# The remaining half of a nested product, with the low halves of probabilities kept in place

## Chip, cores and metric

One core of a Trainium2 chip. The metric is the device time of one execution in microseconds, the median of several runs. Five engines matter: TensorE (PE; its weight loads are listed as PEld), VectorE (DVE), ScalarE (ACT), GpSimd (POOL), and SyncE (SP), which issues all DMAs here.

## The reference

Two branches read the same `x` (2048 tokens, 576 features, float32) and are mixed by a gate per token:

```python
g = _sigmoid((x * gate_w).sum(-1, keepdims=True))
a = _A_ref(x, A_wq, A_wk, A_wv, A_wo, A_beta)   # 32 heads of 18, four segments of 512 tokens:
                                                # causal softmax inside a segment, plus a memory
                                                # read from the segments before it, then @ wo
b = _B_ref(x, B_w_gate, B_w_up, B_w_down)       # (gelu(x @ w_gate) * (x @ w_up)) @ w_down
return g * a + (1 - g) * b                      # w_gate, w_up: 576 x 4608; w_down: 4608 x 576
```

## The kernel before

**Numbers.** All large products run on TensorE in float16. Each operand is written as a high half and a low half (value minus high half); a product is three matmuls, high-high, high-low and low-high. ACT makes the high halves (an activation with `Copy`), and POOL or DVE makes the low halves by subtraction.

**Stages.** First come the projections to queries, keys and values and the memory of the segments (to about 208 us). Then the main loop, to about 1460 us: 72 calls of `step(v)`, in which the gated network and the attention run side by side. A tail applies `wo` and stores the result.

**The gated network.** The 4608 hidden columns form 36 blocks `f` of 128, and the tokens form four chunks of 512. `step(v)` treats block `f = v // 2` for the chunk pair `p = v % 2` (chunks 0 and 1, or 2 and 3). Inside a step the gate and up products for two chunks and two halves of the 576 features (256 features each, and a rest of 64) are done as a 2 x 2 block product in the Winograd form, with seven products instead of eight: `product(...)` with the weight parts A11, A12, A22, S1 to S4. They go to the PSUM banks V, X (bank "G") and Y (bank "U"). Two blocks form a pair `fb = v // 4`, and `i4 = v % 4` counts the steps of one turn: step 0 is the even block with chunks 0 and 1, step 1 the even block with chunks 2 and 3, steps 2 and 3 the odd block.

**The nested term.** One of the seven products, A12 times the second half of the features, is itself taken over two neighbouring blocks (even and odd `f`) and two halves of the chunk (256 tokens), again in seven products instead of eight: `nested(...)`, line 380, each three matmuls of 256 columns. Five of the seven run in the even block's step and two in the odd block's. In the kernel before this is done for the chunk pair 2 and 3 alone (`p == NP`, with `NP = 1`); the pair 0 and 1 does the whole `product(X, f, A12, x1, 2, 6)` in both steps. The sums of the nested form come back through a tile `nest_u[p]` on DVE: five operations of 256 columns in the even step (lines 1384 to 1388), two of 512 columns in the odd step (1397 and 1398), where the plain path has one copy of 512 columns (1402). The first block pair (`fb = 0`) does not nest.

**Weights of the next blocks**, prepared during the steps. POOL scales them (`scale_g`, `scale_up`, `scale_d`, lines 304, 310 and 425 by the profile), forms the Winograd sums (`sums_g`, lines 401 to 405), the nested sums (`nest_sums`, line 324, and a third one, line 421) and the low halves (`low_g`, line 417, `nest_low`, line 337, `low_d`, line 433); ACT makes the high halves. Lines of helpers are those of their last statement in the profile.

**Down products.** `chains` and `down` (line 1222) multiply the hidden values of the pair before by `w_down` (tile `paird`) in the gaps of a step, and DVE adds each into `acc` (line 1230).

**Attention.** Unit `a` is one head in one segment of 512 tokens; `step(v)` with `k = v - 4` starts the scores of units 2k and 2k + 1. `scores` gives four products (query blocks 3 to 0 of 128 rows, with up to 512 keys). DVE adds the mask, finds the maximum and writes the float32 row tile `pf` (line 1133, called `put` in the step, piece by piece: 1, 0, 3, 2). ACT takes the exponentials in place (`powers`, line 1146). `pair_rows` makes the halves: ACT the high half, POOL the low half (line 1157), both into a tile `ph` of two parts. `turn_rows` transposes both by DMA (line 1163), and `values` (line 1177) multiplies by the value rows. There are two `pf` and two `ph` buffers, so unit a + 2 uses those of unit a again.

**Order.** The order of instructions on PE, ACT, DVE and POOL is the order of the program text (`manual_schedule`). Each of these engines runs its list in that order and stops at an instruction whose inputs or target are not ready. The order of SP's DMAs is set by the framework.

Of the kernel before, what the change touches and what calls it, by code (L numbers as in the profile page):

```python
# [18 lines left out]
P = 128  # L19
# [4 lines left out]
L = 512  # L24
# [5 lines left out]
NP = 1  # L30
# [7 lines left out]
GB = 18  # L38
# [8 lines left out]
def kernel(ctx: ExitStack, tc: tile.TileContext, xs, wqk, wv, wo, wgu, wd, beta, out):  # L47
# [264 lines left out]
    A_11, A_12, A_22, N3, N1, N2, N4 = 2, 3, 3, 17, 17, 18, 19  # L312
# [94 lines left out]
    def high_g(f, b):  # L407
        if f < NF and not b:
            pair_g[f] = pair_tile(f)
        for p in parts_g(f, b):  # L410
            act.activation(spot(f, *p, 0), raw_g[f][:, p[0] : p[1]], AF.Copy)  # L411
            if b and f % 2 == 0 and f and p[0] == 0:
                nest_high(f)

    def low_g(f, b):
        for p in parts_g(f, b):
            pool.tensor_tensor(spot(f, *p, 1), raw_g[f][:, p[0] : p[1]], spot(f, *p, 0), OP.subtract)  # L417
            if b and f % 2 == 0 and f and p[0] == 0:
# [650 lines left out]
    with tc.tile_pool(name="keep", bufs=2, side="right", reuse_waits="tile") as kp, ExitStack() as tail:  # L1069
# [7 lines left out]
        home.update(a=ap_, n=stay.enter_context(tc.tile_pool(name="nest", bufs=1, reuse_waits="tile")))  # L1077
# [38 lines left out]
        COL = [0, P, 3 * P, 6 * P, 10 * P]  # L1116
# [3 lines left out]
        def scores(a):  # L1120
# [4 lines left out]
            prob[a] = ap_.tile([P, 10 * P], F32, name="pf", bufs=2)  # L1125
# [6 lines left out]
            def piece(qi):  # L1132
                dve.tensor_tensor_reduce(prob[a][:, COL[qi] : COL[qi + 1]], out[qi], mask[:, L - (qi + 1) * P :],  # L1133
# [4 lines left out]
        def powers(a):  # L1138
# [5 lines left out]
            for qi in (3, 0, 2, 1):  # L1144
                r = p[:, COL[qi] : COL[qi + 1]]
                act.activation(r, r, AF.Exp, bias=b[:, qi : qi + 1], scale=esc[:, 0, c : c + 1])  # L1146

        def pair_rows(a, i):

            p = prob[a]  # L1150
            if i == 0:
                pairs16[a] = ap_.tile([P, 2, 10 * P], F16, name="ph", bufs=2)
                turned_p[a] = ap_.tile([P, 20, P], F16, name="pt", bufs=2)
            h = pairs16[a]
            cols = (slice(6 * P, 10 * P), slice(0, 6 * P))[i]
            act.activation(h[:, 0, cols], p[:, cols], AF.Copy)  # L1156
            pool.tensor_tensor(h[:, 1, cols], p[:, cols], h[:, 0, cols], OP.subtract)  # L1157

        def turn_rows(a):
            prob.pop(a)  # L1160
            t, h = turned_p[a], pairs16.pop(a)
            for i in range(2):
                sp.dma_start(t[:, 10 * i : 10 * i + 10], h[:, i], transpose=True)
# [112 lines left out]
        def weights_first(fb, i4):  # L1276
# [3 lines left out]
            if i4 == 1 and fb:  # L1280
                sums_g(n0 + 1)
            if i4 == 2 and fb:
                scale_g(n0 + 2)
                scale_d(n0)
            if i4 == 3 and fb:
                sums_g(n0 + 2)
                scale_d(n0 + 1)

        def weights_high(fb, i4):
            n0 = 2 * fb  # L1290
            high_g(n0 + 1 + i4 // 2, i4 % 2)
            if i4 == 0:
                nest_high(n0 + 1)
            if i4 >= 2:
                high_d(n0 + i4 - 2)

        def weights_low(fb, i4):
            n0 = 2 * fb
            low_g(n0 + 1 + i4 // 2, i4 % 2)
            if i4 == 0:  # L1300
                nest_low(n0 + 1)
            if i4 >= 2:
                low_d(n0 + i4 - 2)
# [47 lines left out]
        def step(v):  # L1351
# [15 lines left out]
            if v == 3:  # L1367
                high_g(2, 1)
                low_g(2, 1)
            if v in (1, 3 + NP):  # L1370
                nest_high_x(NP, v > 1)
# [3 lines left out]
            if fb and p == NP and f % 2 == 0:  # L1375
# [3 lines left out]
                nested(X[:, n1], f, N1, p, "t1", True)  # L1379
                nested(X[:, n0], f, A_11, p, "b11")  # L1380
# [8 lines left out]
            elif fb and p == NP:  # L1389
# [9 lines left out]
            else:  # L1399
                product(X, f, A11, x1, 0, 4, True)  # L1400
                put(2 * k - 1, 3)
# [3 lines left out]
            if v != 4 and (p != NP or f % 2 == 0):  # L1405
# [20 lines left out]
            if v == 0:  # L1426
                nest_load(NP)
# [27 lines left out]
            if v in (1, 3 + NP):  # L1455
                nest_low_x(NP, v > 1)
# [4 lines left out]
            if v == 0 or fb > 1 and i4 == 1:  # L1461
# [9 lines left out]
            if not fb or p != NP:  # L1471
# [8 lines left out]
            if v == 5:  # L1480
                scales(2)
                scales_out(2)
                scale_up(5)
# [329 lines left out]
```

## Time and profile before

| | |
|---|---|
| median of 3 runs (lowest to highest) | 1566.31 us (1565.99 to 1567.05) |
| the profiled execution, its own time | 1566.07 us |
| span of its trace | 1564.3 us |
| granted TensorE clock | 1.00 |
| busy: DVE, ACT, POOL | 1198.3, 1184.2, 1292.5 us |
| mean traffic of the DMA queues | 134 GB/s, 472452 packets |

In the profile a timeline row reads: start, duration, engine, line, operation, target <- sources, shapes, count, and in brackets the idle time of the engine before it with what ended it. PE rows overlap, since a matmul's duration includes the way through the array; how fast PE goes is read from start to start. A wait row reads: engine, line <- what it waited for: us in total, times, longest. Shares of busy time are averages over stages with different limits. A main-loop turn of four steps takes about 73 us, and the loop is very regular, so one turn stands for seventeen.

### The profile page before, as it was taken

To read this page: it belongs to the slowest core of one execution; us is meant where nothing else is said; L and a number is where in the kernel's file an instruction comes from. 1 tells how busy PE (TensorE), PEld (TensorE's weight loads), DVE (VectorE), ACT (ScalarE), POOL (GpSimd) and SP (SyncE) were. 2 spreads that over 40 slices of the span, in tenths; PEclk is the share of its full clock that TensorE was granted. 3 is DMA by queue.
4 is the path that set the end of the run, shared out by engine and by line. 5 is a ranking of instruction groups with operands and counts; after the bars stand their busy time and mean duration, and the time that the engine had idled before them with its cause. 6 is when DMAs were issued, how large, how long until landed. Compare 5 with 4: busy or idle time off the path is not lost.

```text
span 1564.3 us, 33336 instructions
## 1 busy us (share of the span) xinstructions
PE 1555.5 (99%) x12042; PEld 939.8 (60%) x12043; DVE 1198.3 (77%) x3111; ACT 1184.2 (76%) x2035; POOL 1292.5 (83%) x1309
## 2 busy tenths in 40 slices
PE   9999999999999999999999999999999999999999
PEld 5665655555565555556555555656555556555577
DVE  6788975777878777778787787878787878787665
ACT  7567544888888888887888888888887888876421
POOL 3545776989898989898898989898989898898697
PEclk9999999999999999999999999999999999999999
DMA  7533341787878698978878998989797989884654
GB/s 240 208 131 122 126 136 38 123 135 125 136 128 154 117 144 123 148 122 134 134 132 128 135 139 134 146 122 158 123 139 127 153 118 145 128 136 90 132 111 137
DMA packets 472452, 209.55 MB, mean 134 GB/s; under 512 B 427616, under 2 KB 437344, under 8 KB 471776
## 3 DMA queue, kind: packets, MB, share of 16 engines
q1 hardware_dynamic: 472288, 207.44, 73.7%
q8 instruction: 94, 1.54, 0.4%
q14 instruction: 70, 0.57, 0.1%
HBM read 91.51 MB, written 27.26 MB: 76 GB/s over the span
## 4 chain that ended last, share of the span: by engine, by line
PE 54%; POOL 26%; ACT 12%; issue 6%; DVE 2%; DMA 1%; SPq 0%; POOLq 0%; DVEq 0%
PE dn L1222 13%; PE U L1262 11%; POOL ph L1157 5%; PE V L1262 5%; POOL hh L1249 5%; POOL raw L304 4%; POOL rawd L425 3%; ACT pf L1146 3%; POOL pairg L417 3%; ACT L1146 3%; PE st L440 3%; PE G L1262 2%; PE dn L447 2%; PE pv L1177 1%; ACT gl L1252 1%
## 5 line engine op out<-in xcount | busy, mean ns | idle before, releaser
L1222 PE MATMUL dn<-paird,hh 128*128 128x288 f16 x3396 | 478.8, 286 | 3.2 <-POOL paird L433 3.0
L1157 POOL TENSOR_TENSOR ph<-pf,ph 128x512 f16<-128x512 f32 (+1 forms) x256 | 353.9, 1404 | 114.8 <-ACT ph L1156 108.0
L1262 PEld LDWEIGHTS <-pairg 128*128 128x128 f16 x2820 | 264.0, 98 | 279.0 <-issue 18.0
L1222 PEld LDWEIGHTS <-hh 128*128 128x128 f16 x3456 | 332.1, 98 | 151.9 <-issue 24.5
L1230 DVE SCALAR_TENSOR_TENSOR acc<-dn,ev,acc 128x288 f32<-128x288 f32 x534 | 274.5, 515 | 57.9 <-PE dn L1222 48.0
L1146 ACT ACTIVATE pf<-pf,mb,esc 128x512 f32<-128x512 f32 (+3 forms) x512 | 293.0, 642 | 5.8
L1262 PE MATMUL U<-xt,pairg 128*128 128x512 f16 x864 | 209.9, 379 | 0.0
L417 POOL TENSOR_TENSOR pairg<-raw,pairg 128x640 f16<-128x640 f32 (+2 forms) x144 | 176.5, 1242 | 2.7 <-ACT pairg L411 2.5
L1249 POOL TENSOR_TENSOR hh<-gl,hh 128x512 f16<-128x512 f32 x144 | 164.5, 1163 | 11.5 <-ACT hh L1248 11.5
L1156 ACT ACTIVATE ph<-pf 128x512 f16<-128x512 f32 (+1 forms) x256 | 172.4, 720 | 0.0
L1133 DVE CUSTOM_DVE_ANT_0 pf<-st,mask 128x512 f32<-128x512 f32 (+1 forms) x256 | 157.2, 614 | 0.0
L1262 PE MATMUL U<-x,pairg 128*128 128x512 f16 x636 | 154.6, 379 | 0.1
L411 ACT ACTIVATE pairg<-raw 128x640 f16<-128x640 f32 (+2 forms) x144 | 89.4, 646 | 75.2 <-POOL raw L405 55.6
L1449 DVE COPY gl<-U 128x512 f32<-128x512 f32 x72 | 49.6, 689 | 115.8 <-POOL hh L1249 78.0
L1252 ACT ACTIVATE gl<-gl,sc 128x512 f32<-128x512 f32 x144 | 96.6, 715 | 34.8 <-DVE gl L1491 18.5
L1133 DVE CUSTOM_DVE_ANT_0 pf<-dn,mask 128x256 f32<-128x256 f32 (+1 forms) x192 | 67.2, 375 | 69.0 <-PE dn L1130 68.9
L304 POOL TENSOR_SCALAR raw<-raw,sc 128x640 f32<-128x640 f32 x72 | 118.7, 1661 | 0.0
L1262 PE MATMUL G<-x,pairg 128*128 128x512 f16 x456 | 110.8, 379 | 0.0
L1262 PE MATMUL V<-xt,pairg 128*128 128x512 f16 x432 | 105.7, 381 | 0.0
L1262 PE MATMUL V<-x,pairg 128*128 128x512 f16 x432 | 104.8, 378 | 0.0
L1143 ACT ACTIVATE mb<-mx,esc 128x4 f32<-128x4 f32 x128 | 37.3, 291 | 79.1 <-DVE mx L1133 79.1
L1248 ACT ACTIVATE hh<-gl 128x512 f16<-128x512 f32 x144 | 82.6, 615 | 16.1 <-DVE gl L1244 16.1
(354 smaller groups left out, 2913.8 us busy)
## 6 DMA issues: line engine op xcount, KB each, us to landing
raw<-in_wgu_dram SPq DMA_DIRECT2D x36, 640.0 KB
rawd<-in_wd_dram SPq DMA_DIRECT2D x36, 288.0 KB
qk<-stage SPq DMA_DIRECT2D x36, 256.0 KB
qt<-qk SPq DMA_DIRECT2D x128, 72.0 KB
kt<-qk SPq DMA_DIRECT2D x128, 72.0 KB
vp<-vstage SPq DMA_DIRECT2D x16, 296.0 KB
vt<-vp SPq DMA_DIRECT2D x16, 296.0 KB
qt<-qk SPq DMA_DIRECT2D x128, 36.0 KB
```

The source lines that it names most:

```text
L304: pool.tensor_scalar(r, r, scl[f // 2][0][:, 0:1], None, OP.mult)
L411: act.activation(spot(f, *p, 0), raw_g[f][:, p[0] : p[1]], AF.Copy)
L417: pool.tensor_tensor(spot(f, *p, 1), raw_g[f][:, p[0] : p[1]], spot(f, *p, 0), OP.subtract)
L1133: dve.tensor_tensor_reduce(prob[a][:, COL[qi] : COL[qi + 1]], out[qi], mask[:, L - (qi + 1) * P :], 1.0, -3e38, OP.add, OP.max, mx[a][:, q ...
L1146: act.activation(r, r, AF.Exp, bias=b[:, qi : qi + 1], scale=esc[:, 0, c : c + 1])
L1156: act.activation(h[:, 0, cols], p[:, cols], AF.Copy)
L1157: pool.tensor_tensor(h[:, 1, cols], p[:, cols], h[:, 0, cols], OP.subtract)
L1222: pe.matmul(o[:, :NH], hh[:, a, q * P : (q + 1) * P], w[:, b, n * NH : (n + 1) * NH], start=i == 0, stop=i == 5)
L1230: dve.scalar_tensor_tensor(av, o[:, :NH], ev, av, OP.mult, OP.add)
L1249: pool.tensor_tensor(hh[:, 1], t, hh[:, 0], OP.subtract)
L1252: act.activation(t, o, AF.Gelu_apprx_tanh, scale=scl[f // 2][0][:, 2 + c : 3 + c])
L1262: pe.matmul(o, w[:, i, (a + k) * P : (a + k + 1) * P], x[:, b + k], start=start and k == 0 and i == 0 and b == h, stop=k == 1 and i == 1, ...
```

## The change

1. The nested form is used for both chunk pairs. The constant `NP` goes, and with it the plain path in all block pairs but the first. Chunks 0 and 1 get their own words (`nest_load`, `nest_form`, `nest_high_x`, `nest_low_x` for p = 0 and 1) and their own tiles. In an odd block the nested weight sum N3 is written over the part of A12 that nothing reads any more (`N3 = 2`, `GB = 17`).
2. The low half of the probabilities is written into the first half of the bytes of `pf`, in place, so that `ph` has one part. The columns of `pf` are reversed: query block 3 lies first and block 0 last. The low half is transposed first, then the high half.
3. The order on POOL and ACT: `scale_d` for both blocks goes to the middle of step 1, behind `scales_out` and `scale_up`; the sums of the odd block go from step 1 to the end of step 0; in step 3 the second block's down weights and the nested halves are made between the two parts of `high_g` and `low_g`, and the third nested sum comes last.

```diff
-NP = 1
-GB = 18
+GB = 17
...
-    A_11, A_12, A_22, N3, N1, N2, N4 = 2, 3, 3, 17, 17, 18, 19
+    A_11, A_12, A_22, N3, N1, N2, N4 = 2, 3, 3, 2, 17, 18, 19
...
+    def nest_third(f):
+        if f < NF:
+            s3 = nest_w[f + 1] = nest_u[1][:, NL : NL + P]
+            pool.tensor_tensor(s3, raw_g[f + 1][:, KW + 3 * P : KW + 4 * P], nest_w[f][:, P : 2 * P], OP.subtract)
...
-        r = nest_x[p, "r"] = home["a"].tile([P, 10 * P], F32, name="pf", bufs=2)
+        r = nest_x[p, "r"] = home["p"][p]
...
-    def low_g(f, b):
+    def low_g(f, b, between=lambda: None):
+        if f >= NF:
+            between()
         for p in parts_g(f, b):
             pool.tensor_tensor(spot(f, *p, 1), raw_g[f][:, p[0] : p[1]], spot(f, *p, 0), OP.subtract)
-            if b and f % 2 == 0 and f and p[0] == 0:
-                nest_low(f)
-                s3 = nest_w[f + 1] = nest_u[NP][:, NL : NL + P]
-                pool.tensor_tensor(s3, raw_g[f + 1][:, KW + 3 * P : KW + 4 * P], nest_w[f][:, P : 2 * P], OP.subtract)
+            if p[0] == 0 and b:
+                between()
...
-        home.update(a=ap_, n=stay.enter_context(tc.tile_pool(name="nest", bufs=1, reuse_waits="tile")))
+        home.update(p=[ap_.tile([P, 10 * P], F32, name=f"pf{i}", bufs=1) for i in range(2)], n=stay.enter_context(tc.tile_pool(name="nest", bufs=1, reuse_waits="tile")))
...
-        COL = [0, P, 3 * P, 6 * P, 10 * P]
+        COL = [9 * P, 7 * P, 4 * P, 0]
...
-            prob[a] = ap_.tile([P, 10 * P], F32, name="pf", bufs=2)
+            prob[a] = home["p"][a % 2]
...
-            for qi in (3, 0, 2, 1):
+            for qi in (3, 2, 1, 0):
...
-                pairs16[a] = ap_.tile([P, 2, 10 * P], F16, name="ph", bufs=2)
+                pairs16[a] = ap_.tile([P, 10 * P], F16, name="ph", bufs=2)
...
-            cols = (slice(6 * P, 10 * P), slice(0, 6 * P))[i]
-            act.activation(h[:, 0, cols], p[:, cols], AF.Copy)
-            pool.tensor_tensor(h[:, 1, cols], p[:, cols], h[:, 0, cols], OP.subtract)
+            cols = (slice(0, 4 * P), slice(4 * P, 10 * P))[i]
+            act.activation(h[:, cols], p[:, cols], AF.Copy)
+            pool.tensor_tensor(p.bitcast(F16)[:, cols], p[:, cols], h[:, cols], OP.subtract)
...
-            prob.pop(a)
-            t, h = turned_p[a], pairs16.pop(a)
-            for i in range(2):
-                sp.dma_start(t[:, 10 * i : 10 * i + 10], h[:, i], transpose=True)
+            t = turned_p[a]
+            for i, h in ((1, prob.pop(a).bitcast(F16)[:, : 10 * P]), (0, pairs16.pop(a))):
+                sp.dma_start(t[:, 10 * i : 10 * i + 10], h, transpose=True)
...
-            if i4 == 1 and fb:
-                sums_g(n0 + 1)
             if i4 == 2 and fb:
                 scale_g(n0 + 2)
-                scale_d(n0)
             if i4 == 3 and fb:
                 sums_g(n0 + 2)
-                scale_d(n0 + 1)
...
-            low_g(n0 + 1 + i4 // 2, i4 % 2)
+            low_g(n0 + 1 + i4 // 2, i4 % 2, lambda: (low_d(n0 + 1), nest_low(n0 + 2)) if i4 == 3 else None)
             if i4 == 0:
                 nest_low(n0 + 1)
-            if i4 >= 2:
-                low_d(n0 + i4 - 2)
+                sums_g(n0 + 1)
+            if i4 == 2:
+                low_d(n0)
+            if i4 == 3:
+                nest_third(n0 + 2)
...
-            if v in (1, 3 + NP):
-                nest_high_x(NP, v > 1)
+            if 1 <= v < 5:
+                nest_high_x((v - 1) % 2, v > 2)
...
-            if fb and p == NP and f % 2 == 0:
+            if fb and f % 2 == 0:
...
-                nested(X[:, n1], f, N1, p, "t1", True)
-                nested(X[:, n0], f, A_11, p, "b11")
+                nested(X[:, n0], f, A_11, p, "b11", True)
+                nested(X[:, n1], f, N1, p, "t1")
...
-            elif fb and p == NP:
+            elif fb:
...
-                nest_load(NP)
+                for n in range(2):
+                    nest_load(n)
...
                     scale_up(2 * fb + 3)
+                    scale_d(2 * fb)
+                    scale_d(2 * fb + 1)
                 else:
-                    nest_form(NP)
+                    nest_form(0)
...
                 hidden_pair(f, c, g0)
+                if v == 1:
+                    nest_form(1)
                 ahead[v + 1] = first_product(v + 1)
```

`high_g` and `weights_high` change as `low_g` and `weights_low` do, for ACT.

More of the change, by code (lines that the diff above doesn't have):

```diff
@@ L1132, in piece @@
             def piece(qi):
-                dve.tensor_tensor_reduce(prob[a][:, COL[qi] : COL[qi + 1]], out[qi], mask[:, L - (qi + 1) * P :],
+                dve.tensor_tensor_reduce(prob[a][:, COL[qi] : COL[qi] + (qi + 1) * P], out[qi], mask[:, L - (qi + 1) * P :],
                                          1.0, -3e38, OP.add, OP.max, mx[a][:, qi : qi + 1])
@@ L1404, in step @@
                 scale_result()
-            if v != 4 and (p != NP or f % 2 == 0):
+            if v != 4 and i4 < 2:
                 some(fb - 1, early[:1])
@@ L1483, in step @@
                 scale_up(5)
+                scale_d(2)
+                scale_d(3)
             product(Y, f, S1, t, 0, 2)
```

26 lines of the change are left out of this document (15 added, 11 removed).

## Prediction

> **What bounds the kernel now.** I read the page first (busy shares), then a table of windows cut at the steps of the main loop, then PE's list of waits, then the timelines of PE, POOL, DVE and SP over the same four steps.
>
> ```profile
> span 1564.3 us, 33336 instructions
> PE 1555.5 (99%) x12042; PEld 939.8 (60%) x12043; DVE 1198.3 (77%) x3111; ACT 1184.2 (76%) x2035; POOL 1292.5 (83%) x1309
> ```
>
> TensorE is busy all the time, so a microsecond is won only where PE has fewer columns to push, or where it stands still inside that 99%. The windows are cut where each step's first product (into V) starts. In order they are step 3 of one turn of the loop (odd block, chunks 2 and 3), then steps 0 (even block, chunks 0 and 1), 1 (even, 2 and 3) and 2 (odd, 0 and 1) of the next.
>
> ```profile
> 597.56:615.16 17.60, 17.60 (x150) 10.60 (x147) 13.89 (x38) 14.49 (x25) 17.07 (x19) 1.00 0.82 116
> 615.16:633.76 18.60, 18.41 (x149) 10.59 (x146) 13.52 (x37) 17.11 (x32) 16.55 (x15) 1.00 0.86 132
> 633.76:652.39 18.63, 18.63 (x159) 11.51 (x157) 16.94 (x48) 14.54 (x24) 14.97 (x20) 1.00 1.14 157
> 652.39:670.63 18.24, 18.24 (x149) 10.60 (x146) 13.07 (x37) 15.85 (x28) 16.62 (x13) 1.00 0.75 130
> ```
>
> Columns: length, then busy us of PE, PEld, DVE, ACT, POOL, then clock and DMA. A turn is 73.07 us at full clock (1.00). Steps 0 and 2 run the same products now (149 matmuls each), yet step 0 is 0.36 us longer. Steps 1 and 3 already have the nested term that the change brings to steps 0 and 2, so they show what steps 0 and 2 should become. POOL is 17.07 us busy out of 17.60 in step 3: it, not DVE or ACT, is the engine next to PE.
>
> ```profile
> PE dn L1222 <- POOL paird L433: 3.0, 16, 0.2
> ```
>
> PE's only repeated wait, once per turn from the second turn on: the down chain needs the low half of a block's down weights.
>
> **The change, part by part.**
>
> *The term in seven products, chunks 0 and 1.*
>
> ```profile
> 618.61 0.41 PE L1222 MATMUL dn<-paird,hh 128*128 128x288 f16 x2 [0.19 <-POOL paird L433]
> ...
> 635.07 0.82 PE L380 MATMUL G<-x,pairg 128*128 128x256 f16 x6
> ...
> 636.05 1.46 PE L1262 MATMUL U<-x,pairg 128*128 128x512 f16 x6
> ...
> 653.70 1.46 PE L1262 MATMUL G<-x,pairg 128*128 128x512 f16 x6
> 654.99 0.90 PE L1222 MATMUL dn<-paird,hh 128*128 128x288 f16 x6
> ```
>
> Six matmuls of 512 columns take 654.99 - 653.70 = 1.29 us, 0.215 each. From 635.07 to 636.05 PE runs nine nested matmuls of 256 columns (six into G, three into dn): 0.98 us, 0.109 each, so half the columns cost half the time. Step 0 loses one product (1.29) and gets five nested ones, 15 matmuls (1.64): +0.34. Step 2 loses 1.29 and gets two, six matmuls (0.65): -0.64. The windows agree: step 3 (nested) is 17.60 against 18.24 for step 2 (not), and step 1 against step 2 is +0.39, a little of it the scale sum that only step 1 has. Net -0.30 us a turn; the nested path runs for 17 of the 18 block pairs (not the first): **-5.1 us**. Nine weight loads more per turn lie beside matmuls (PEld 11.51 us of 18.63 in step 1).
>
> DVE pays:
>
> ```profile
> 618.14 0.69 DVE L1402 COPY U<-G 128x512 f32<-128x512 f32 x1
> ...
> 622.48 0.69 DVE L1449 COPY gl<-U 128x512 f32<-128x512 f32 x1 [2.44 <-POOL hh L1249]
> ...
> 637.01 0.42 DVE L1384 COPY nu<-G 128x256 f32<-128x256 f32 x1
> ...
> 639.00 0.43 DVE L1388 TENSOR_TENSOR G<-U,nu 128x256 f32<-128x256 f32 x1
> ```
>
> In step 0 one copy of 0.69 becomes five operations from 637.01 to 639.43, 2.4 us: +1.7. In step 2 it becomes two additions of 512 columns, +0.7. In front of L1449 DVE idles 2.44 us in step 0, and the added work falls just there, ahead of the same copy; DVE then holds 15.2 of 18.6 us, less than step 1's 16.94, where PE waits for nothing. Priced at nothing; without that cover it would be up to 1.7 us a turn, 29 in all. ACT's exponentials of the odd unit start up to 1.6 us later in step 0, as they do in step 1.
>
> *POOL's order.* Weight products of POOL around step 3, and its two gaps:
>
> ```profile
> 605.54 0.73 POOL L401 TENSOR_TENSOR raw<-raw 128x256 f32<-128x256 f32 x1
> ...
> 608.65 0.46 POOL L405 TENSOR_TENSOR raw<-raw 128x128 f32<-128x128 f32 x1
> 609.08 1.73 POOL L425 TENSOR_SCALAR rawd<-rawd,sc 128x576 f32<-128x576 f32 x1
> 610.78 2.77 POOL L1157 TENSOR_TENSOR ph<-pf,ph 128x512 f16<-128x512 f32 x2
> 613.49 1.42 POOL L417 TENSOR_TENSOR pairg<-raw,pairg 128x640 f16<-128x640 f32 x1
> 614.86 0.93 POOL L337 TENSOR_TENSOR pairg<-junk,pairg 128x384 f16<-128x384 f32 x1
> ...
> 617.27 1.29 POOL L433 TENSOR_TENSOR paird<-rawd,paird 128x576 f16<-128x576 f32 x1
> 618.56 2.77 POOL L1157 TENSOR_TENSOR ph<-pf,ph 128x512 f16<-128x512 f32 x2
> ...
> 636.78 2.77 POOL L1157 TENSOR_TENSOR ph<-pf,ph 128x512 f16<-128x512 f32 x2 [4.92 <-ACT ph L1156]
> ...
> 655.42 2.76 POOL L1157 TENSOR_TENSOR ph<-pf,ph 128x512 f16<-128x512 f32 x2 [1.62 <-ACT ph L1156]
> ```
>
> POOL's work does not grow. The down weights' scaling (L425, 1.73 us) leaves steps 2 and 3 and goes, both together (3.5 us), to the end of step 1. The five weight sums (L401 to L405, 605.54 to 609.11, 3.6 us) go from the head of step 1 to the end of step 0, into the gap of 4.92 us, which still holds them if the odd unit comes 0.9 us later. The head of step 1 is free 3.6 us earlier, so the 3.5 us behind it plus the gap of 1.62 fit ahead of 655.42. In step 3 everything behind L425 comes 1.73 earlier, and L433 moves ahead of the nested and second weight parts. Its end goes from 618.56 to 613.49 + 1.42 - 1.73 + 1.29 = 614.5, three microseconds before the down chain asks. The wait goes: 0.36 us (step 0 against step 2), 16 times: **-5.8 us**.
>
> What is late next: the nested low halves of an even block (L337), which PE needed in step 1 until now and needs in step 0 then, about 616.8 (615.16 + 1.3 for the first product + three nested matmuls). They end at 614.5 + 0.93 = 615.4; slack 1.4 us. Should the 1.73 not come through, 617.1, a wait of 0.3.
>
> *Low halves over the probabilities.* No engine gains or loses an instruction; POOL's subtraction keeps its shape. What changes is the wait: DVE writes the next unit's scores into that buffer, and for the first pieces of the row (query blocks 3 and 2) it must now wait for the transpose of the low half to land, where it waited for POOL. Pieces 1 and 0 lie behind the low halves' bytes. Behind the waiting DVE instruction stand the down chains' sums and the hidden products, so PE soon pays. SP now issues the low half first; with that the high half, ready earlier, also waits for POOL.
>
> ```profile
> 627.45 0.42 DVE L1133 CUSTOM_DVE_ANT_0 pf<-dn,mask 128x256 f32<-128x256 f32 x1 [1.59 <-PE dn L1130]
> ...
> 629.64 0.68 DVE L1133 CUSTOM_DVE_ANT_0 pf<-st,mask 128x512 f32<-128x512 f32 x1
> ```
>
> ```profile
> 622.05 5.51 SPq L1163 DMA_TRANSPOSE pt<-ph  x2
> ```
>
> ```profile
> DMA  6111189991111111111169999900002999131159
> ```
>
> POOL is done with a unit at 618.56 + 2.77 = 621.33, SP issues its two transposes from 622.05, and DVE writes piece 3 two units on at 629.64. The digits are DMA's busy tenths from 622 to 632 us, 0.25 each: the first transpose works around 623.5 to 624.25 and 626.75 to 628.25, the second to 630.5. So the transpose that is issued first has moved its bytes by 628.25, 1.4 us before DVE needs the buffer. How long from the last byte to the waiting engine?
>
> ```profile
> 1467.70 2.27 POOL L1628 TENSOR_TENSOR pairg<-ot 128x512 f32<-128x512 f16 x2 [4.22 <-DMA ot<-orow]
> ```
>
> ```profile
> DMA  6946999985100000499999999998179861669862
> ```
>
> Here POOL does wait for a transpose. The digits run from 1460 us; the activity of its two transposes ends at about 1467.0, and POOL starts 0.7 us later. So 628.25 + 0.7 = 628.95 against 629.64: nothing, with 0.7 us to spare. The Trainium skill (page "DMA: Bandwidth & Descriptors", section "Anatomy of one DMA") says otherwise: about 2 us of fixed cost, most of it behind the last byte until the write is confirmed. By that the buffer would be free at 630.25, 0.6 us late; the trace has 0.7 us where the page has up to 2, on a transpose too, so I go by the trace.
>
> In the odd units of step 3 POOL ends 1.73 earlier, which pays for the low half's way.
>
> *The first block pair.* Chunks 0 and 1 need their own words: one more load of 512 KB (behind the first, needed 15 us later) and four more subtractions on POOL in step 1 of the first pair, put ahead of that step's last low half.
>
> ```profile
> 218.33 1.69 POOL L349 TENSOR_TENSOR nu<-pf 128x256 f32<-128x256 f32 x1 [0.31 <-DMA pf<-in_xs_dram]
> ...
> 221.71 0.72 POOL L349 TENSOR_TENSOR pf<-pf 128x256 f32<-128x256 f32 x1
> ...
> 232.99 2.27 POOL L1249 TENSOR_TENSOR hh<-gl,hh 128x512 f16<-128x512 f32 x2
> ```
>
> ```profile
> 235.74 0.69 DVE L1449 COPY gl<-U 128x512 f32<-128x512 f32 x1 [2.39 <-POOL junk L324]
> ```
>
> ```profile
> 237.20 1.46 PE L1262 MATMUL U<-xt,pairg 128*128 128x512 f16 x6
> ```
>
> The same four took 218.33 to 222.43, 4.1 us; at 0.73 each with small gaps 3.1. They go between the two low halves at 232.99, whose second ends then at 238.4 to 239.4 instead of 235.26. It frees the buffer that DVE's copy at 235.74 writes, and PE's product at 237.20 needs that copy done: 239.1 to 240.1, a stall of 1.9 to 2.9, once. I take **+2.4 us**, since the one slow row of the four may come again. The few ACT and DVE operations on those words fall into idle time there.
>
> **Sum.** -5.1 - 5.8 + 2.4 = -8.5. The profiled execution took 1566.07 us (span 1564.3 and 1.8 around it), 0.24 under the median: 1557.6 in its terms, **1557.8 us** as a median.
>
> **Rivals.**
>
> *Late low half (slower).* One mechanism: piece 3 waits on DVE for the transpose. It decides at 0.7 us more than I reckon from issue to landing. Against it: the rows above, and loads in the queue were already in them. For it: SP's order is not written out by the kernel, so loads may stand ahead of the transposes, and single issues take 3 us where two together took 5.51. If 1 us is added in one unit of each step, DVE is 0.3 late; 64 steps with attention make 19 us: 1577. At 0.14 us a step (8.5 / 64) the gain is gone. Were the wait set for the whole buffer and not for its overlapping bytes, piece 1 at 627.45 would wait for 628.95, 1.5 us, over 90 us in all. Against that:
>
> ```profile
> 660.40 3.74 POOL L304 TENSOR_SCALAR raw<-raw,sc 128x640 f32<-128x640 f32 x2
> ```
>
> ```profile
> 662.42 0.72 ACT L411 ACTIVATE pairg<-raw 128x640 f16<-128x640 f32 x1
> ```
>
> ACT reads the first part of a tile at 662.42 while POOL writes its second until 664.14: waits go by parts.
>
> *The wait moves (no change).* POOL does not run ahead, and the nested low halves are late in step 0 instead of the down weights. Against: in step 3 its work falls from 17.07 to 15.3 us of 17.6. If the wait stays as it is, 5.8 come back: 1563.6; with 0.3 more for the nested ones, 17 times, 1568. I say 1563 to 1568.
>
> *No start cost (faster).* If the stall in the first pair is covered: 1555.4.
>
> **How the numbers follow.** About 0.2%, 3.1 us, is what a measurement of this kernel can tell from no change. Forecast with its bounds (1553.5 to 1563): 0.72, the start cost of nothing to 2.9 and half the wait in it. Wait moves: 0.12, nearly all within 0.2%. Late low half: 0.13 slower; a few more for the moved wait at its worst. So faster 0.73, same 0.12, slower 0.15. The range runs from 1553.5 to 1571, through the moved wait and the mild end of the late half.
>
> **What would show it.** Right: steps 0 to 3 of 18.6, 18.6, 17.6 and 17.6 us; no wait of PE for L433; the gap of 4.92 on POOL filled with the sums; one PE stall of about 2 us near 237. Wrong: DVE's score pieces (L1133) waiting for DMA, with every step longer by the same amount; PE waiting for L337; or steps 0 and 2 not differing as steps 1 and 3 do.

## The result, and the profile after

The changed kernel takes 1556.84 us (median of 6 runs, 1556.42 to 1557.48); the kernel before took 1565.99 beside it (6 runs). The ratio is 0.9941, with a 95% interval of 0.9930 to 0.9953: faster by 9.15 us, where 8.5 were forecast. In every later set of runs the median of the kernel before was 1565.68 to 1566.03, so times of different sets can be compared to a few tenths of a microsecond.

The page after: the span, the busy line, and the line of the chain that ended last, by engine.

```profile
span 1554.5 us, 33926 instructions
...
PE 1548.9 (100%) x12195; PEld 955.6 (61%) x12196; DVE 1229.6 (79%) x3198; ACT 1183.8 (76%) x2037; POOL 1306.2 (84%) x1313
...
PE 94%; POOL 3%; ACT 2%; DVE 1%; issue 1%; POOLq 0%
```

TensorE issues 153 matmuls more and is busy for 6.6 us less, because more of them are half as wide. The span fell by 9.8 us, so the other 3.2 are time in which TensorE stood still. In the windows view, cut as for the kernel before (steps 3, 0, 1, 2), this is plain:

```profile
595.91:613.52 17.61, 17.61 (x149) 10.61 (x147) 13.89 (x38) 14.43 (x25) 16.09 (x18) 1.00 0.69 118
613.52:632.12 18.60, 18.60 (x159) 11.50 (x156) 14.82 (x41) 17.23 (x32) 16.06 (x16) 1.00 0.77 146
632.12:650.74 18.62, 18.62 (x159) 11.50 (x157) 16.61 (x48) 14.46 (x24) 16.33 (x21) 1.00 0.83 137
650.74:668.35 17.61, 17.61 (x150) 10.61 (x147) 13.89 (x38) 15.83 (x28) 17.45 (x13) 1.00 0.71 139
```

In the second row length and PE's busy time are now equal (18.60 and 18.60, before 18.60 and 18.41): the products grew by as much as the wait shrank. The fourth row is 0.63 shorter than before. Steps 0 and 1 are alike, and so are steps 2 and 3. PE's list of waits has no repeated entry left:

```profile
PE G L783 <- POOL wst L779: 1.0, 1, 1.0
PE U L1268 <- DVE G L1396: 0.4, 1, 0.4
PE G L447 <- DVE wp L128: 0.3, 1, 0.3
```

Over all turns, the starts of each step's first product in the two traces give this account of the span, in us (the first of the 72 steps starts at 208.2 in both, the last at 1471.9 before and 1462.2 after, so the loop reaches beyond the 1460 us named above):

| part | before | after | difference |
|---|---|---|---|
| start of the main loop to its fifth step | 41.47 | 41.88 | +0.4 |
| fifth step (first with the nested term in its place) | 19.19 | 20.18 | +1.0 |
| the other 16 of step 0 | 297.07 | 297.02 | -0.05 |
| step 1, 17 of them | 315.66 | 315.21 | -0.45 |
| step 2, 17 of them | 308.62 | 298.02 | -10.60 |
| step 3, 16 of them | 281.66 | 281.70 | +0.04 |
| all else | 300.6 | 300.5 | -0.1 |

Together -9.8 us in the two profiled executions, against -9.15 by medians.

POOL's timeline from step 3 to the head of step 1:

```profile
610.41 1.40 POOL L426 TENSOR_TENSOR pairg<-raw,pairg 128x640 f16<-128x640 f32 x1
611.78 1.28 POOL L440 TENSOR_TENSOR paird<-rawd,paird 128x576 f16<-128x576 f32 x1
613.02 0.91 POOL L336 TENSOR_TENSOR pairg<-junk,pairg 128x384 f16<-128x384 f32 x1
...
616.92 2.89 POOL L1164 TENSOR_TENSOR pf<-pf,ph 128x512 f16<-128x512 f32 x2 [1.45 <-ACT ph L1163]
...
631.11 0.73 POOL L406 TENSOR_TENSOR raw<-raw 128x256 f32<-128x256 f32 x1
...
634.61 0.46 POOL L410 TENSOR_TENSOR raw<-raw 128x128 f32<-128x128 f32 x1
635.14 2.89 POOL L1164 TENSOR_TENSOR pf<-pf,ph 128x512 f16<-128x512 f32 x2
```

The low half of the down weights (L440, before L433) ends 0.46 us before step 0 begins at 613.52; before, it ended 3.4 us after that step's start. The five sums, 631.11 to 635.07, fill the old gap of 4.92 us, and the nested low half (L336) ends at 613.93, 0.9 us before PE's first nested product of the step (614.83). Lines of the changed kernel have other numbers than those before: L426 was L417, L336 was L337, L440 was L433, L406 to L410 were L401 to L405, L1164 was L1157.

### The profile page after: what moved, and what is told of

It is laid out like the page before. It is cut to its first block, busy times and chain, and to the rows that moved or that the text cites. A ratio compares the mean times of both kernels' runs of the same rounds, so it can differ in the third digit from the quotient of the medians.

```text
span 1554.5 us, 33926 instructions
## 1 busy us (share of the span) xinstructions
PE 1548.9 (100%) x12195; PEld 955.6 (61%) x12196; DVE 1229.6 (79%) x3198; ACT 1183.8 (76%) x2037; POOL 1306.2 (84%) x1313
## 4 chain that ended last, share of the span: by engine, by line
PE 94%; POOL 3%; ACT 2%; DVE 1%; issue 1%; POOLq 0%
PE dn L1228 27%; PE U L1268 22%; PE V L1268 12%; PE pv L1183 4%; PE G L385 3%; PE st L447 3%; PE dn L454 2%; PE U L1275 2%; PE dn L385 1%; PE U L447 1%; PE V L1280 1%; PE G L1280 1%; PE G L447 1%; PE st L1137 1%; PE st L1667 1%; PE V L1275 1%
## 5 line engine op out<-in xcount | busy, mean ns | idle before, releaser
L1164 POOL TENSOR_TENSOR pf<-pf,ph 128x512 f16<-128x512 f32 (+1 forms) x256 | 359.3, 1403 | 95.0 <-ACT ph L1163 84.1
L1268 PEld LDWEIGHTS <-pairg 128*128 128x128 f16 x2616 | 244.0, 98 | 255.6 <-issue 19.2
L1268 PE MATMUL U<-x,pairg 128*128 128x512 f16 x840 | 204.1, 379 | 0.0
L426 POOL TENSOR_TENSOR pairg<-raw,pairg 128x640 f16<-128x640 f32 (+2 forms) x144 | 176.3, 1240 | 3.5 <-ACT pairg L418 1.9
L1183 PEld LDWEIGHTS <-pt 128*128 128x128 f16 x2560 | 83.4, 96 | 12.3
```

The source lines that it names most:

```text
L1164: pool.tensor_tensor(p.bitcast(F16)[:, cols], p[:, cols], h[:, cols], OP.subtract)
L1183: pe.matmul(ov, pr[:, 10 * i + COL[qi] // P + kb], v[:, 4 * e + kb, c0 : c0 + VC], start=kb == 0 and i == 0, stop=kb == qi and i == 1)
L1268: pe.matmul(o, w[:, i, (a + k) * P : (a + k + 1) * P], x[:, b + k], start=start and k == 0 and i == 0 and b == h, stop=k == 1 and i == 1, ...
```

## The experiments

The theory going in: two gains on TensorE that do not depend on each other, the nested products (0.30 us a turn net) and the wait of the down chain (0.36), a start cost, and nothing for writing the low halves over the probabilities. Each run undoes or does one part. The nested term by itself was not run; its share is read from the lengths of the steps.

**The order of POOL alone**, on the kernel before (the third part of the change only):

```diff
+                    scale_d(2 * fb)
+                    scale_d(2 * fb + 1)
...
-            if i4 == 1 and fb:
-                sums_g(n0 + 1)
...
+            low_g(..., lambda: (low_d(n0 + 1), nest_low(n0 + 2)) if i4 == 3 else None)
```

> The kernel before with the new order on POOL and ACT alone (scaling of the down weights in step 1, odd block's sums at the end of step 0, down halves ahead of the nested ones in step 3); term and probabilities as before. Theory: the order alone takes away PE's wait for the low down weights, 0.36 us in 16 turns, and nothing else: 1566.0 - 5.8 = 1560.2, step 0 at 18.24 instead of 18.60, no wait of PE for line 433's operation. Rival (the two parts need each other): without the shorter turn POOL's relief is worth nothing and the time stays at 1566, or the nested halves, made later in step 3, are late and it rises over 1566.

Measured: 1561.68 (ratio 0.9973, 0.9963 to 0.9983), 1.5 us more than expected. Step 0 fell from 18.604 to 18.257 and its sum by 5.5 us: the repeated wait is gone, as the theory says. POOL's busy time in step 3 is 15.37 us (15.3 reckoned). Step 1, though, is 1.3 us longer in all. A single wait of 1.1 us, in the sixth step of the loop, is most of it and does not return in the full change. Besides, step 1 is 0.02 to 0.06 us longer in 14 of the turns: the sums that now lie at the end of step 0 hold up an operation of DVE there (0.95 to 0.98 us, before 0.81), which is the subject of the last experiment.

**The old order, the rest of the change kept:**

> The changed kernel with the old order on POOL and ACT; nested term for all chunks and low halves over the probabilities stay. Theory: the nested term saves its 5 us and costs about 1 us at the start, and the wait for the low down weights stays: 1556.8 + 5.8 = 1562.6; it may grow, since a turn is 0.3 us shorter while POOL has the same to do in steps 2 and 3 (16.6 and 17.1 us of 17.6): up to 0.6 us more a turn, 1572. Rival (order worth nothing, the saving is in the columns): 1557.

Its edit is the reverse of the one above, on the changed kernel. Measured: 1564.24 (0.9991, 0.9982 to 1.0000). So 7.4 us of the gain need the order. In the profiled execution (its runs spread from 1561.72 to 1566.43, and this is the shortest) steps 1 to 3 are as in the full change, so step 2 has the gain of the nested term here too; step 0 is 18.91 instead of 18.60, 5.3 us in all. What the longer runs have besides stays open. PE's wait does not stay with the down weights. It is now in step 0's first product, as POOL's timeline (first) and PE's show:

```profile
614.25 1.40 POOL L422 TENSOR_TENSOR pairg<-raw,pairg 128x640 f16<-128x640 f32 x1
```

```profile
615.00 1.75 PE L1266 MATMUL V<-xt,pairg 128*128 128x512 f16 x6
```

The product needs the low half that POOL finishes at 615.65, after the product has begun; its six matmuls take 1.75 us where they take 1.47 elsewhere. The stall sits inside a group of matmuls, in gaps of 0.10 to 0.15 us, and the list of waits counts one of them (0.2) in the whole execution: a group longer than its like is where to look.

**Low halves over the probabilities alone**, on the kernel before (second part only):

```diff
-            pool.tensor_tensor(h[:, 1, cols], p[:, cols], h[:, 0, cols], OP.subtract)
+            pool.tensor_tensor(p.bitcast(F16)[:, cols], p[:, cols], h[:, cols], OP.subtract)
```

> The kernel before with the low halves written over the probabilities alone (reversed columns, one-part high tile, new order of the two transposes). Theory: no instruction more or less, and DVE's piece 3 comes after the low half has landed, so nothing: 1566.0, within 0.2%; no row of DVE's scores waiting for a DMA. In the kernel before the second transposes of units landed as late as the time of piece 3 in one class of units, so up to 0.5 us in one step of four, 8 us, is possible: 1574. Rival (the in-place half is itself part of the gain, by quicker transposes): 1560 to 1564.

Measured: 1572.87 (1.0043, 1.0030 to 1.0055): slower by 7 us. That is within the 8 us that the expectation allowed, but mostly for another reason. In PE's waits the entry of the down weights is not 3.0 us, as it was, but

```profile
PE dn L1221 <- POOL paird L433: 7.4, 16, 0.5
```

and DVE's waits have a new one:

```profile
DVE pf L1133 <- DMA pt<-pf: 7.6, 12, 1.1
```

Step 0 carries 5.3 of the 7 us, step 1 1.7. Nothing got longer on POOL but one thing: the two subtractions of a unit take 2.89 us where they took 2.77 (compare the rows of L1164 above with L1157 before). Each by itself is as long as it was. In place, the second writes bytes which the first reads, and in the trace it carries a wait for POOL's own semaphore, in every unit, which it does not before; it starts 0.08 us after the first has ended, where it started 0.04 before that end. That is 0.12 us a unit, two units in step 3, 0.24 of step 0's 0.27. So POOL is the path there in the old order, and the price of the in-place form hangs on the order.

The rest can be told turn by turn. DVE's waits for the transpose fall into longer steps in four places, 1.1 us in all. Three of the steps 1 (0.5 to 0.9 us longer each) follow a step 0 at whose end DVE's subtraction into `oh` takes 1.12 to 1.22 us instead of 0.81, beside a low half on POOL: the subject of the last experiment. The kernel before has one such turn, 0.58 us.

**Only the down weights' place in step 3**, on the kernel before (their low half ahead of the nested and second parts, their high half on ACT likewise, no scaling moved):

```diff
             if b and f % 2 == 0 and f and p[0] == 0:
+                if f > 2:
+                    low_d(f - 1)
                 nest_low(f)
```

> The kernel before with one edit of the order alone: in step 3 the second down block's high and low halves are made ahead of the nested halves; the scaling of the down weights and the sums stay where they were. Theory: the low half then ends at 613.5 + 1.4 + 1.3 = 616.2 of the old timeline, before PE asks at 617.8; nested halves are needed only a step later there. The whole wait goes: 1560.2, the same as with the full order. Rival (the wait is one of POOL's load, so only moving the 1.7 us of scaling out of step 3 helps): 1566.

Measured: 1567.06 (1.0002, 0.9993 to 1.0010): nothing won. Step 0 loses its wait here too (18.257), and step 1 gives all of it back, 6.4 us, in three turns. Its runs spread from 1564.19 to 1568.28. PE's waits and ACT's timeline at one of them:

```profile
PE G L380 <- DVE gl L1248: 3.6, 3, 1.6
```

```profile
553.91 0.74 ACT L95 ACTIVATE junk<-raw 128x640 bf16<-128x640 f32 x1 [2.98 <-DMA raw<-in_wgu_dram]
...
560.22 1.33 ACT L1256 ACTIVATE gl<-gl,sc 128x512 f32<-128x512 f32 x2
```

ACT stands 2.98 us for a block of raw weights; its gelu, further back in its queue, is late, then DVE's operation behind that, then PE. The raw buffer comes free with the second part's low half, which is the operation that was pushed back. That last link is read from the code and the trace, not tried by itself.

**Only the scaling put back**, the rest of the new order kept:

```diff
             if i4 == 2 and fb:
                 scale_g(n0 + 2)
+                scale_d(n0)
             if i4 == 3 and fb:
                 sums_g(n0 + 2)
+                scale_d(n0 + 1)
```

> The changed kernel with only the scaling of the down weights put back to steps 2 and 3, all other moves of GpSimd's order kept. Theory: taking 1.73 us out of step 3 is the essential part of the new order. With it back, the low half of the third weight part ends about 0.3 us after TensorE's first product wants it and the nested low half ends about 1.6 us later than now, at 615.5, where TensorE wants it at 614.8: up to 0.9 us a turn, 16 turns, 1561 to 1571, and TensorE's waits name the nested or the third part's low half. Rival: the other moves already leave room, and nothing changes: 1557.

Measured: 1572.2 (1.0040, 1.0027 to 1.0052), just above the upper end: step 0 is 19.59, +1.0, in 15 of 16 turns. PE's waits name the nested low half, and its timeline shows that of six nested matmuls it is the last that waits:

```profile
PE G L385 <- POOL pairg L336: 7.9, 15, 0.5
```

```profile
692.45 0.71 PE L385 MATMUL G<-x,pairg 128*128 128x256 f16 x5
693.68 0.28 PE L385 MATMUL G<-x,pairg 128*128 128x256 f16 x1 [0.53 <-POOL pairg L336]
```

Five of them starting 0.109 us apart would have the sixth start at 692.99; it starts 0.69 later. Another 0.3 us a turn is again inside the first product (1.77 us for six matmuls), which makes up the 1.0. So the exchange alone, the run before this, moves the wait, and without the 1.73 us taken out of step 3 the full order is a loss too. What taking them out would give without the exchange was not run.

**The start cost: four subtractions on DVE instead of POOL.**

```diff
-            pool.tensor_tensor(o, a, b, OP.subtract)
+            (dve if p else pool).tensor_tensor(o, a, b, OP.subtract)
```

In the changed kernel DVE's timeline in the first pair has

```profile
235.83 0.69 DVE L1457 COPY gl<-U 128x512 f32<-128x512 f32 x1 [2.39 <-PE U L1268]
...
247.63 0.69 DVE L1457 COPY gl<-U 128x512 f32<-128x512 f32 x1 [3.40 <-POOL hh L1255]
```

so the copy that the prediction had waiting, the first, waits for TensorE alone, and the same copy one step on waits for POOL.

> The changed kernel with the four subtractions that form the words of chunks 0 and 1 (second step of the first pair) on VectorE instead of GpSimd. In the changed kernel's trace they hold GpSimd from 234.10 to 237.23, the low half of the hidden pair behind them ends at 238.34, and one step on VectorE's copy waits for it (idle 3.40 us ahead of 247.63) and TensorE stands still 0.4 us at 248.0. Theory: that is what the start costs, so the chain goes and the fifth step starts at 249.7 again: 1556.4. If the extra 0.6 us of the first nested step hangs on the same lateness too, 1555.8. Rival: four more operations of 0.4 us on VectorE delay its own copies by as much, and nothing is won: 1556.8 or a little more.

Measured: 1556.57 (0.9942, 0.9930 to 0.9955): no difference from the change, so the rival holds. The copy at 247 no longer waits for POOL, but DVE's timeline starts with the moved work:

```profile
231.75 0.85 DVE L354 TENSOR_TENSOR pf<-pf 128x256 f32<-128x256 f32 x1
232.53 0.68 DVE L1339 COPY gl<-V 128x512 f32<-128x512 f32 x1
```

The copy behind it frees the bank of PE's next product, and PE loses 0.5 us there instead (0.4 of it in its list of waits). The fifth step starts 42.1 us into the loop, against 41.9, and takes 20.17 us, as in the changed kernel, so the extra time in it does not hang on POOL's lateness. There, in the changed kernel, PE waits for DVE's last nested addition:

```profile
257.57 1.45 PE L1268 MATMUL U<-xt,pairg 128*128 128x512 f16 x6 [0.40 <-DVE G L1396]
```

In that step PE has neither down products nor attention products ahead of this product, and so it comes to it earlier.

**How much room DVE has in step 0.** DVE was priced at nothing. In the changed kernel its timeline and PE's say 0.73 us: from 619.12, the end of the last addition, to 619.85, the product that writes the bank it reads.

```profile
618.69 0.43 DVE L1396 TENSOR_TENSOR G<-U,nu 128x256 f32<-128x256 f32 x1
```

```profile
619.85 1.46 PE L1268 MATMUL U<-xt,pairg 128*128 128x512 f16 x6
```

Two kernels repeat the addition ahead of it, once and four times:

```diff
                 dve.tensor_tensor(u[:, n1], X[:, n1], u[:, n0], OP.add)
+                for _ in range(n):
+                    dve.tensor_tensor(u[:, n1], X[:, n1], u[:, n0], OP.add)
```

> The changed kernel with one more addition of 256 columns on VectorE (a repeat of the fourth, 0.46 us with its gap) ahead of the last one of step 0, once a turn, 17 times. VectorE's last addition there ends at 619.12 and TensorE's next product into the same buffer starts at 619.85: 0.73 us apart. Theory: 0.46 fits, 1556.8, with VectorE's idle time of 1.41 us behind it shrinking to about 0.95. Rival: the hand-over between the engines takes more than 0.27 us of the 0.73, and TensorE waits 0.1 to 0.3 us, 17 times: 1558.5 to 1562.

> The changed kernel with four such repeats, 1.84 us a turn on VectorE ahead of the last addition of step 0. Theory: only 0.73 us of it is covered there, the other 1.1 is TensorE's: 17 times, 1576, with TensorE waiting for VectorE's fifth addition ahead of its product into U. If the hand-over takes 0.2 us of the cover, 1579. Rival: the idle time of VectorE in the step (1.41 us before the next copy, more elsewhere) takes it in, under 4 us in all: 1557 to 1561.

Measured: 1564.89 (0.9992, 0.9983 to 1.0001) and 1599.13 (1.0213, 1.0199 to 1.0227). Both expectations fall. One slip is of counting: the branch runs in steps 0 and 1, so 34 times and not 17. For four repeats that explains most of it:

```profile
PE U L1268 <- DVE G L1398: 37.4, 34, 2.2
```

that is 1.1 us each, 1.84 less the 0.73: the cover was read rightly. But one repeat, 0.46, fits under it and still costs 8 us. Step 0 is unchanged (18.597; only the fifth step, which has no cover, takes the whole 0.46) and step 1 is 0.44 longer, all of it at its head, where PE has no wait listed. There the slow thing is an operation of DVE at the end of step 0, the attention's subtraction into `oh` (L1212), of which both inputs lie in SBUF: 1.36 us, where it is 0.90 in the changed kernel and 0.81 in the one before, in 14 of 15 turns. Behind it DVE reads the bank that PE's plain product into U writes next; in the changed kernel it ends 0.08 us ahead of that product (706.76 to 706.84):

```profile
706.02 0.74 DVE L1250 SCALAR_TENSOR_TENSOR gl<-U,sc,gl 128x512 f32<-128x512 f32 x1
```

```profile
706.84 0.81 PE L1268 MATMUL U<-x,pairg 128*128 128x512 f16 x3
```

Where PE does wait there, in all the runs of this section, it starts 0.05 us after DVE's end, so only 0.03 of the 0.08 is to spare. New theory: the repeat makes ACT and POOL 0.46 later, so POOL's first weight sum starts just as DVE's subtraction does, and the two shut each other out. Four kernels tell this from a DVE that is simply full: the time on DVE placed where nobody waits for it, the repeat in step 0 alone, that with POOL's sums put 0.43 us earlier, and the latter with no time added.

```diff
+            if fb and not i4:
+                dve.tensor_copy(X[:, n1], X[:, n1])
```

> The changed kernel with one more operation of 256 columns on VectorE (0.42 us, a copy of a part of the sum onto itself) once a turn in step 0 only, placed behind the score piece of 384 columns, just ahead of the 1.41 us in which VectorE waits for TensorE. Theory: an addition ahead of the last sum costs 0.44 us a turn not by VectorE's time but by making ScalarE, and with it GpSimd, 0.46 later, so that GpSimd's first weight sum begins just before VectorE's subtraction of two SBUF operands at the end of step 0, which then takes 1.36 us where it takes 0.90 now; TensorE's product into U at the head of step 1 has only 0.07 us to spare behind it. Placed here, the same time on VectorE makes nobody late: 1557. Rival: VectorE is simply full in step 0, and any 0.42 us on it costs that much: 1563 to 1564.

```diff
+                if not i4:
+                    dve.tensor_tensor(u[:, n1], X[:, n1], u[:, n0], OP.add)
```

> The changed kernel with the one repeated addition of 0.46 us ahead of the last sum in step 0 only. Theory: the loss of the kernel that has it in steps 0 and 1 comes from step 0's alone, all of it at the head of step 1: 1556.8 + 16 x 0.44 = 1564, step 1 at 19.06. Rival: step 1's own addition makes it, and here the time stays at 1557.

```diff
-                nest_low(n0 + 1)
                 sums_g(n0 + 1)
+                nest_low(n0 + 1)
```

> As the kernel before it in this list (one repeated addition in step 0), and GpSimd's five weight sums at the end of step 0 put ahead of the odd block's nested low half (0.43 us) instead of behind it; no work more or less. Theory: the sums then begin 0.43 earlier, VectorE's subtraction starts in the middle of the first of them as it does in the changed kernel and takes 0.90 us again: the 0.44 a turn goes, 1557. Rival: it is not the sums' place but VectorE's own time: 1564.

> The changed kernel with only that exchange on GpSimd and nothing added on VectorE. Theory: the second sum (1.13 us) now begins at about 776.4 in the turn shown, as VectorE's subtraction does. If GpSimd has the port first, the subtraction ends 0.5 to 0.9 us later and TensorE pays 16 times: 1565 to 1570. If VectorE has it first, it takes 0.81 us, and the time is 1557 or a little less. Rival: GpSimd's order has no say in VectorE's time, 1557.

| kernel | us | ratio to before (95%) | step 1, us |
|---|---|---|---|
| changed | 1556.84 | 0.9941 (0.9930 to 0.9953) | 18.62 |
| copy behind the pieces | 1556.49 | 0.9940 (0.9926 to 0.9954) | 18.63 |
| repeat in step 0 | 1563.1 | 0.9982 (0.9973 to 0.9991) | 19.06 |
| the same, sums earlier | 1559.5 | 0.9958 (0.9945 to 0.9970) | 18.79 |
| sums earlier, no repeat | 1556.67 | 0.9940 (0.9927 to 0.9952) | 18.62 |

The second and third rows settle it between the theories: about the same time on DVE (0.42 and 0.46) costs nothing where it delays nobody, and 6.3 us where it does. (The kernel with the repeat in both steps has, besides, single waits of 0.9 us in the sixth step and 1.2 us in one step 2; they were not followed.) The order of two POOL operations takes 3.6 of these back, less than expected: it brings the sums forward by 0.26 us (from 0.55 to 0.81 ahead of step 1) and not by 0.43. What that does is to be seen in the subtraction and the first sum, in one turn each. Before (DVE; POOL has nothing there):

```profile
706.28 0.81 DVE L1206 SCALAR_TENSOR_TENSOR oh<-ob,wsc,oh 128x576 f16<-128x576 f32 x1
```

The repeat in step 0, DVE and POOL:

```profile
706.47 1.36 DVE L1212 SCALAR_TENSOR_TENSOR oh<-ob,wsc,oh 128x576 f16<-128x576 f32 x1
```

```profile
706.48 0.73 POOL L406 TENSOR_TENSOR raw<-raw 128x256 f32<-128x256 f32 x1
```

The same with the sums earlier:

```profile
705.27 1.09 DVE L1212 SCALAR_TENSOR_TENSOR oh<-ob,wsc,oh 128x576 f16<-128x576 f32 x1
```

```profile
705.02 0.72 POOL L406 TENSOR_TENSOR raw<-raw 128x256 f32<-128x256 f32 x1
```

The changed kernel:

```profile
703.99 0.90 DVE L1212 SCALAR_TENSOR_TENSOR oh<-ob,wsc,oh 128x576 f16<-128x576 f32 x1
```

```profile
703.54 0.73 POOL L406 TENSOR_TENSOR raw<-raw 128x256 f32<-128x256 f32 x1
```

DVE begins 0.01 us before, 0.25 and 0.45 after POOL's sum, and takes 0.55, 0.28 and 0.09 longer than 0.81. Offset and excess add up to 0.54, 0.53 and 0.54: DVE gets nowhere until 0.54 us after the start of POOL's operation. In the first case 0.46 more than the changed kernel's 0.90, less the spare of 0.03, gives 0.43 a turn (0.44 measured), in the second 0.19 less 0.03 gives 0.16 (0.17 measured). With the sums earlier and no repeat, DVE is first and POOL pays:

```profile
703.92 0.81 DVE L1212 SCALAR_TENSOR_TENSOR oh<-ob,wsc,oh 128x576 f16<-128x576 f32 x1
```

```profile
704.01 1.31 POOL L407 TENSOR_TENSOR raw<-raw 128x256 f32<-128x256 f32 x1
```

POOL's sum takes 1.31 us, where the like of it next to nobody takes 0.73. The time alone, 1556.67, does not part this from the rival that POOL's order has no say; the rows do, and the 3.6 us above. No kernel here is faster than the changed one by more than the 0.2% that can be told.

## Why the prediction was right, point by point

- **The nested term, -5.1.** Its sizes on TensorE stand. Step 2 fell by 0.637 in the median (0.64 forecast), and step 0, with the wait gone, is 18.60 as step 1 is.
- **The wait for the down weights, -5.8.** It went, and POOL's low half ended at 613.06, 0.46 us before step 0; I had it 0.7 before. The order alone gives 4.1, the order within the change 7.4, because without it the other two parts make POOL's lateness worse. The split of the gain into terms that simply add was too simple, and the sum came out because all three parts were done.
- **What is late next.** The nested low halves had 1.4 us to spare by the prediction; in the trace they end at 613.93, and the sixth nested matmul, which needs them, starts at 614.83 + 5 x 0.109 = 615.4: as forecast. Its warning, "Should the 1.73 not come through", is the run with the scaling put back: I reckoned a wait of 0.3 there; it was 0.7, and the third weight part's low half, late as well, made it 1.0 a turn. The rival *the wait moves* is real and was priced too low for that case.
- **Low halves over the probabilities, nothing.** This step failed in its reason and held in its outcome, by the help of another part. "POOL's subtraction keeps its shape" is true of each operation; the pair no longer overlaps, and POOL pays 0.12 us a unit. The new order hides it: POOL has 1.5 to 2.5 us idle in steps 3, 0 and 1 of the changed kernel (0.16 in step 2). In the old order the second part by itself costs 7 us. The spare time of 0.7 us for piece 3 was read wrongly. In the row of digits shown, the last busy slice of the first transpose ends at 628.5 and not at 628.25, and the semaphore of the transpose issued at 622.05 had its last update at 629.88, 0.24 us after piece 3 began (629.64): in the old order there was nothing to spare. That update came 1.4 us behind the last busy slice, twice the 0.7 that the prediction went by and nearer to the 630.25 that it set aside. So the rival *late low half* is real there (7.6 us of DVE's waits, 12 times, 1.1 us of time). In the changed kernel it stayed away: over 126 units the first score piece starts 1.07 us or more after the last update for the low half that it overwrites. SP's order is not the reason, for "SP now issues the low half first" holds in the trace for 61 of 128 units; the framework orders SP's queue. POOL's earlier end, which the prediction names for the odd units, is the likely one and was not tried by itself.
- **The start, +2.4.** Mis-sized, and for the wrong buffer. The copy at 235.8 does not wait for POOL's late operation, which ended at 238.34; the copy one step on waits for the hidden low halves of its own step, and TensorE stops for 0.3 us at about 248. All that the start lost is 0.4 us before the fifth step. The fifth step has another 0.65 beyond the nested term's 0.34, but 0.57 of it is DVE's work and not the start's. Against the terms of the sum the profiled executions are 1.3 us better at the start and in the fifth step together and 0.45 in single waits of step 1 that went, and 0.6 worse in the other steps 0 and 2; so about 1.2 in all, of which the medians show 0.65 (9.15 against 8.5).
- **DVE at nothing.** Right for 16 turns, by a hair, and wrong for the first: in the fifth step PE waits for DVE's nested additions (0.40 us listed, 0.57 by the distance of the matmuls' starts). The reason given, 2.44 us of idle time ahead of a copy and a busy share below step 1's, says nothing of the end of the step, where 0.03 us is left. Nor does "without that cover up to 29" name that danger: 0.46 us too much on DVE was covered ahead of the copy and still cost 6 to 8, by the meeting with POOL.

## What to carry to other kernels

An idle gap in an engine's timeline covers added work only as far as that engine itself goes: also follow what the added work makes late on other engines, to the next place where they meet. When a part of a change is priced at nothing because something hides it, test it without the rest of the change; here that part alone was a loss of 7 us. Look for stalls inside groups of matmuls too: six that take 1.75 us instead of 1.47 are a wait that the list hardly shows.

## What the runs showed of the hardware

A VectorE operation with two SBUF inputs and a GpSimd operation shut each other out. A subtraction on VectorE with two SBUF inputs (128x576) takes 0.81 us with GpSimd idle. Begun beside a GpSimd addition of 256 columns, 0.01 us before its start or 0.25 or 0.45 us after it, it gets nowhere until 0.54 us after that start; beside a GpSimd low half of 0.91 us, in three turns of the kernel with the low halves over the probabilities and in one of the kernel before, until 0.72. Both are 0.19 us short of the end of the GpSimd record. When the subtraction begins 0.09 us or more ahead, it takes its 0.81, and the GpSimd addition takes 1.31 instead of 0.73. The Trainium skill (page "SBUF — State Buffer", section "Who interferes with whom") states this: a VectorE instruction with two SBUF inputs and a GpSimd instruction that reads SBUF share a port pair, and whichever issues first blocks the other. The runs agree, in both directions, but for the start 0.01 us ahead, where the records put VectorE first and it is VectorE that waits.

Two GpSimd operations in a row overlap by about 0.04 us at their seam where the second waits for nothing on its own engine. Where it waits for GpSimd's own semaphore, as in the in-place form, it starts 0.08 us after the first has ended, and the pair took 2.89 us instead of 2.77.
